# Seven blocks of a fused attention and two-MLP kernel: a table of start times becomes one written order, and the attention product of a head pair two matmuls

## The chip, the cores and the metric

The kernel runs on one core of one Trainium2 chip. The metric is the device time of one execution in microseconds (us). The profile was taken of one execution of the kernel before the change; its own time stands in the table below beside the median of three runs.

## What is computed

```python
def _attn_ref(q, k, v):                       # (8, 8, 576, 64) each
    q_s = q - np.max(q, axis=-1, keepdims=True)
    q_s = np.exp(q_s)
    q_s = q_s / (np.sum(q_s, axis=-1, keepdims=True) + 1e-09)
    k_s = k - np.max(k, axis=2, keepdims=True)
    k_s = np.exp(k_s)
    k_s = k_s / (np.sum(k_s, axis=2, keepdims=True) + 1e-09)
    kv = np.einsum('bhsd,bhse->bhde', k_s, v)
    return np.einsum('bhsd,bhde->bhse', q_s, kv)
...
    x = attn_out as 4608 rows of 512
    g = x @ w_gate;  val = x @ w_val           # 512 x 1536 each
    y = (g * sigmoid(g) * val) @ w_out         # 1536 x 512
    h = y @ w_in;  solu = h * softmax(h)       # 512 x 1024
    out = layernorm(solu) * g_ln @ w_out2      # 1024 x 512
```

All in float32. Each large product is made of three matmuls on float32r parts of its operands, high by high, high by low and low by high.

## The kernel before

The 4608 rows are nine **blocks** of 512. Block 0 runs in an opening that is written out by hand, and prepares block 1. Blocks 1 to 7 run in a steady loop. Block 8 and a tail (the second MLP, about 440 us) follow. The change touches blocks 1 to 7.

On TensorE a block is 36 **groups** of 12 matmuls of 512 columns: for each of the 12 slices i of the hidden width **g_i** (x times the gate weights, tile wg), **v_i** (x times the value weights, tile wv) and **o_i** (the product times the output weights, accumulated in the four banks y). g and v write in turn to four PSUM banks (the class Slots deals them out); so do the small tiles px and pk below. Before the change they run g_i, o_(i-2), v_i.

Between them stands the work for the block that follows, and other work that the block carries:
- **g and v**: ScalarE makes Silu of wg into a tile st (L891, three buffers). VectorE multiplies st by wv (L896), ScalarE rounds it to its high part a (L900, two buffers), VectorE subtracts for the low part (L902). Then o_i can run.
- **k and v of batch j+1**, four heads at a time: loads (kv_load, v_load), column maxima and subtraction on VectorE (kv_max_rows, kv_max_all), exp on ScalarE (kv_exp), 40 small matmuls into two pk tiles (kv_mm, L525), then scaling on VectorE and ScalarE into the 128x128 tiles kvh and kvl of each head pair, with the two heads' 64x64 blocks on the diagonal.
- **q of block j+1**: softmax over 64 (q_max, q_exp, q_norm), a transposing DMA (q_turn), then for each of four head pairs its parts qhl (q_split), and **x** of the pair (x_mm): three matmuls kvh by q high, kvh by q low, kvl by q high, for each batch that the 512 columns touch. A block that spans two batches has six matmuls a pair, a block in one batch three.
- **y of block j-1**: copied out of its banks (y_keep), seven forms made and stored (y_form).
- **w2**: one of eight pieces of the second MLP's weights is loaded raw (w2_raw), put together by two ScalarE instructions (L186, L187) and two on VectorE, and stored.
- **weights**: nine slices f of the gate and value weights are streamed from DRAM in each block, 1 MB each, through three buffers (stream_next), and the w2 piece takes a turn in them.

All DMAs are issued by SP, in program order; every engine runs its instructions in program order. Before the change the order comes from a table of start times: `at(t, n, ...)` puts a step behind the n-th of the 36 groups.

Of the kernel before, what the change touches and what calls it, by code (L numbers as in the profile page):

```python
# [18 lines left out]
P = 128  # L19
# [17 lines left out]
x2 g11 x3 x2 kvn v10 v11 s11 b8 x2 co5 o9 n2 g11 qnx co5 v10 v11 v11 v11 o10  # L37
""".split()


class Task:

# [1 line left out]
    current = None  # L44

    def __init__(self, f, a):
        self.f, self.a, self.g, self.done = f, a, None, False

    def step(self):
        before, Task.current = Task.current, self  # L50
# [13 lines left out]
    def next(self):  # L64
        self.step()
# [16 lines left out]
def attention_glu_solu_kernel(  # L82
# [46 lines left out]
    def f32(ap):  # L129
        return ap.bitcast(F32)  # L130
# [380 lines left out]
    def kv_mm(ps, pool, b, h0, u):  # L511
        pr = h0 // 2 + u
        need(pr in k_done if b == 0 else (b, h0) in kt_exp)
        pk = ps.tile([P, D + 1], F32, tag="gv", name="pk")
        heads = [2 * u + a for a in range(2)]
        if b:
            kt, vt = (t[b, h0][:, 0:NT_, :].rearrange("p (h c) d -> p h c d", c=LC) for t in (kt_t, vt_t))
            parts = [[(kt[:, h, c, :], vt[:, h, c, 0:D + 1]) for h in heads] for c in range(LC)]
            parts.append([(kt_t[b, h0][:, NT_ + u, :], vt_t[b, h0][:, NT_ + h, 0:D + 1]) for h in heads])
        else:  # L520
            kt, vt = kt_t[b, h0][1], vt_t[b, h0]
            parts = [[(kt[:, c, h, :], vt[:, h, c, 0:D + 1]) for h in heads] for c in range(KC)]
        for c, pair in enumerate(parts):
            for a, (kk, vv) in enumerate(pair):
                nc.tensor.matmul(  # L525
                    out=pk[a * D:(a + 1) * D, :], lhsT=kk, rhs=vv, start=c == 0, stop=c == len(parts) - 1
                )
        yield
        hi, lo = kv_parts[b % 2, pr]
        rs = stat.tile([P, 1], F32, tag="rs", bufs=4, name="rs")  # L530
        nc.vector.tensor_scalar_add(out=rs, in0=pk[:, D:D + 1], scalar1=1e-9)
        nc.vector.reciprocal(out=rs, in_=rs)
        yield
        diag = [slice(a * D, (a + 1) * D) for a in range(2)]
        for s in diag:
            nc.scalar.activation(out=hi[s, s], in_=pk[s, 0:D], func=AF.Copy, scale=rs[s])
        yield
        for s in diag:
            nc.vector.scalar_tensor_tensor(
                out=lo[s, s], in0=pk[s, 0:D], scalar=rs[s], in1=f32(hi[s, s]),  # L540
                op0=ALU.mult, op1=ALU.subtract,
            )
        kv_done.add((b, pr))

    kv_done = set()

    def segments(j):

# [107 lines left out]
    def q_turn(pool, j):  # L656

        n = BLOCKS[j][1] // 4
        w = tmp.tile([n, 2, 4 * H * D], U16, tag="yt", bufs=1, name="qw")
        parts = qt_t[j][1].bitcast(U16).rearrange("p c h (d w) -> p c h d w", w=2)  # L660
        wo = w.rearrange("p w (c h d) -> p w c h d", c=4, h=H)
        nc.vector.tensor_copy(out=wo[:, 0], in_=parts[:, :, :, :, 0])
        nc.scalar.copy(out=wo[:, 1], in_=parts[:, :, :, :, 1])
        qw_t[j] = wT = pool.tile([P, 2, 4, NPAIR, n], U16, tag="qt", bufs=1, name="qwT")
        nc.sync.dma_start_transpose(
            out=wT.rearrange("e w c r p -> e (w c r) p"), in_=w.rearrange("p w n -> p (w n)")
        )

    def q_split(pool, j, pr):

        wT, n = qw_t[j], BLOCKS[j][1]
        z = pool.tile([P, n], F32, tag="z", bufs=1, name="z")
        for half, copy in enumerate((nc.vector.tensor_copy, nc.scalar.copy)):
            copy(
                out=halves(z)[half].rearrange("e (c p) -> e c p", c=4), in_=wT[:, half, :, pr, :]
            )
        qh, ql = q_parts(pool, n)
        nc.scalar.copy(out=qh, in_=z)
        nc.vector.tensor_tensor(out=ql, in0=z, in1=f32(qh), op=ALU.subtract)
        qT_t[j, pr] = (qh, ql)  # L680

    xs = {}

    def x_tiles(xpool, j):
        xs[j] = [
            xpool.tile([P, KD, BLOCKS[j][1]], F32R, tag=f"{n}{j % 2}", name=n)
            for n in ("xh", "xl")
        ]

    def x_mm(ps, j, pr):  # L690
        qh, ql = qT_t.pop((j, pr))
# [36 lines left out]

    def tasks_of(j):

        t = {}
        b = j + 1
        if b < B:
            for n, (load, rows, sub, exp, mm) in enumerate(((0, 2, 5, 9, 11), (12, 17, 20, 24, 26))):
                h0 = n * HG  # L740
                if n:
                    at(t, load, kv_load, b, h0)
                    at(t, load, v_load, b, h0)
                at(t, rows, kv_max_rows, att, b, h0)
                a = Task(kv_max_all, (att, b, h0))
                at(t, sub, a.next)
                at(t, sub + 1, a.finish)
                at(t, exp, kv_exp, b, h0)
                for u in range(2):
                    at(t, mm, kv_mm, ps_at, att, b, h0, u)  # L750
        at(t, 15, lambda: w2_raw[j - 1].start())
        at(t, 23, join_w2, j - 1)
        at(t, 24, parts_of_w2, j - 1)
        if j + 1 < NB:
            m = Task(q_max, (att, j + 1, ALLH, nc.vector, 2))
            n = Task(q_norm, (att, j + 1, ALLH, nc.vector, 2))
            at(t, 8, m.next)
            at(t, 9, m.next)
            at(t, 10, m.finish)
            at(t, 12, q_exp, j + 1, ALLH)  # L760
            at(t, 13, n.next)
            at(t, 14, n.next)
            at(t, 15, n.finish)
            at(t, 18, q_turn, att, j + 1)
            at(t, 24, x_tiles, ph1x, j + 1)
            for p in range(NPAIR):
                at(t, 27 + p, q_split, att, j + 1, p)
                at(t, 29 + p, x_mm, ps_at, j + 1, p)
            at(t, 27, kv_next, j + 1)
            at(t, 33, q_next, j + 1)  # L770
        y_forms_at(t, j - 1)
        for e, f in enumerate(STREAM):
            if f is not None:
                at(t, 3 * f + 2, stream_next, j, e)
        at(t, 24, store_w2, j - 1)
        at(t, 25, stream_next, j, STREAM.index(None))
        return t
# [49 lines left out]
    def y_form(j, n):  # L827


        i, x, with_ = Y_FORMS[n]  # L830
        of = lambda n, r: y_quarter(j, n, r)
        if with_:
            if x and with_[0]:
                yz[j] = att.tile([P, 2, KH, P], F32, tag="z", bufs=1, name="yz")
            y_sum(yz[j], of, x, with_)
            s = yz[j]
        else:
            s = of(*x)
        f = att.tile([P, 2, 2, KH * P], F32R, tag="qhl", bufs=2, name="yf")
        h, l = (f[:, n].rearrange("p q (k t) -> p q k t", k=KH) for n in range(2))  # L840
        nc.scalar.copy(out=h, in_=s)
        yield
        nc.vector.tensor_tensor(out=l, in0=s, in1=f32(h), op=SUB)
        nc.sync.dma_start(out=yf_dram[j, i], in_=f32(f))

    def y_forms_at(t, j):


        tasks = [Task(y_form, (j, n)) for n in range(7)]
        for n, g in enumerate((4, 6, 8, 11, 12, 14, 16)):  # L850
            at(t, g, tasks[n].step)
            at(t, g + 1, tasks[n].finish)

    acts = {}
# [15 lines left out]

    ys = {}

    def emit_o(j, i, start, stop):
        if start:
            for t in ps0.held.values():
                t.finish()
            ys[j] = [y_bank(k)[:, :BLOCKS[j][1]] for k in range(KD)]
        ah, al = acts.pop((j, i))
        wh, wl = weight(("wo", i))
        for k in range(KD):  # L880
            s = slice(k * P, (k + 1) * P)
            mm3(ys[j][k], wh[:, s], wl[:, s], ah, al, start, stop)
        if stop and j < NB - 1:
            for k in range(KD):
                y_keep(j, k)

# [7 lines left out]
    def v_rest(j, i, pv):  # L894
        st = acts[j, i]
        nc.vector.tensor_tensor(out=st, in0=st, in1=pv, op=ALU.mult)  # L896
        yield
        a = apool.tile([P, 2, BLOCKS[j][1]], F32R, tag="a", bufs=2, name="a")
        ah, al = a[:, 0], a[:, 1]
        nc.scalar.copy(out=ah, in_=st)  # L900
        yield
        nc.vector.tensor_tensor(out=al, in0=st, in1=f32(ah), op=ALU.subtract)  # L902
        acts[j, i] = (ah, al)
# [38 lines left out]
    class Slots:  # L942
# [4 lines left out]

        def tile(self, shape, dtype, tag, name):
            k = self.at % self.n
            if k in self.held and not self.held[k].done:  # L950
                self.held[k].finish()
            self.at += 1
            self.held[k] = Task.current
# [23 lines left out]
    def opening():  # L977
# [102 lines left out]
        nc.sync.dma_start(out=g_sb, in_=g_ln.rearrange("(c p) -> p c", p=P))  # L1080
        pend.append((0, NF - 1, False, True))

    opening()
    for j in range(1, NB - 1):
        block(j, range(NF), tasks_of(j))
    man.close()


# [415 lines left out]
```

## Time and profile before

| | |
|---|---|
| median of 3 runs | 1350.85 us (1350.08 to 1351.71) |
| the profiled execution's own time | 1350.75 us |
| its span, first to last instruction | 1349.0 us |
| TensorE matmul busy | 1333.8 us, 99% |
| VectorE busy | 874.4 us, 65% |
| ScalarE busy | 688.0 us, 51% |
| mean granted TensorE clock | 0.997 |

A matmul's record lasts longer than the step from one matmul to the next, because they are pipelined. What a matmul costs in a stream is read from the starts: the distance from one start to the next. The profile's waits say which engine waited for which; TensorE's own waits all lie in the opening and the tail.

### The profile page before, as it was taken

How to read it: one execution, taken by the hardware profiler on the slowest of the kernel's cores; microseconds unless marked ns; L12 is line 12 of the kernel's file. 1: busy time of each engine (PE TensorE's matmuls, PEld its weight loads, DVE VectorE, ACT ScalarE, POOL GpSimd, SP SyncE). 2: the span in 40 equal slices, each digit the busy share in tenths (PEclk: the TensorE clock that was granted, in tenths of full speed). 3: DMA queues.
4: the chain of work that ended last, by engine and by line, in shares of the span. 5: the costliest groups of instructions: out<-in, count | busy, mean ns of one | idle time of the engine just before them, and what ended most of it. 6: DMA issues, size and time to landing. Idle time of an engine off the chain costs nothing.

```text
span 1349.0 us, 17478 instructions
## 1 busy us (share of the span) xinstructions
PE 1333.8 (99%) x6646; PEld 1102.4 (82%) x6646; DVE 874.4 (65%) x1513; ACT 688.0 (51%) x967; POOL 34.7 (3%) x134
## 2 busy tenths in 40 slices
PE   7999999999999999999999999999999999999998
PEld 5778888888888888888888888888887888888887
DVE  6999566376376466467367445464288778778774
ACT  5877255245345345344345424442166766766764
POOL 2000000000000000000000000000000000000000
PEclk9999999999999999999999999999999999999999
DMA  9977575476465556564664653564376676686651
GB/s 231 339 264 273 175 240 160 125 238 170 131 216 166 157 192 182 161 196 141 191 206 126 249 182 116 183 234 179 121 184 185 165 204 173 163 200 179 164 141 40
DMA packets 239700, 247.57 MB, mean 184 GB/s; under 512 B 147840, under 2 KB 213376, under 8 KB 228608
## 3 DMA queue, kind: packets, MB, share of 16 engines
q1 hardware_dynamic: 239616, 246.45, 61.0%
q8 instruction: 52, 0.85, 0.3%
q14 instruction: 32, 0.26, 0.1%
HBM read 162.01 MB, written 59.24 MB: 164 GB/s over the span
## 4 chain that ended last, share of the span: by engine, by line
PE 93%; DVE 4%; SPq 1%; issue 1%; DMA 1%; ACT 0%; DVEq 0%; ACTq 0%
PE wg L858 7%; PE y L860 7%; PE y L858 7%; PE y L859 7%; PE wv L858 7%; PE wv L860 7%; PE wv L859 7%; PE wg L860 7%; PE wg L859 7%; PE y L1335 5%; PE y L1334 5%; PE y L1333 5%; PE h L858 4%; PE h L860 4%; PE h L859 4%; PE pk L525 1%
## 5 line engine op out<-in xcount | busy, mean ns | idle before, releaser
L900 ACT CAST a<-st 128x512 fp32r<-128x512 f32 x108 | 66.9, 620 | 332.7 <-DVE st L896 328.1
L896 DVE TENSOR_TENSOR st<-st,wv 128x512 f32<-128x512 f32 x108 | 74.2, 687 | 185.2 <-PE wv L860 183.1
L858 PE MATMUL wg<-xh,wgv 128*128 128x512 f32 x432 | 170.5, 395 | 0.0
L860 PE MATMUL y<-a,wo 128*128 128x512 f32 x432 | 168.5, 390 | 0.7 <-DVE wo L221 0.7
L858 PE MATMUL y<-a,wo 128*128 128x512 f32 x432 | 168.6, 390 | 0.0
L859 PE MATMUL wg<-xl,wgv 128*128 128x512 f32 x432 | 168.5, 390 | 0.0
L858 PE MATMUL wv<-xh,wgv 128*128 128x512 f32 x432 | 168.4, 390 | 0.0
L859 PE MATMUL y<-a,wo 128*128 128x512 f32 x432 | 168.2, 389 | 0.2 <-DVE a L902 0.2
L860 PE MATMUL wg<-xh,wgv 128*128 128x512 f32 x432 | 168.3, 389 | 0.0
L860 PE MATMUL wv<-xh,wgv 128*128 128x512 f32 x432 | 168.1, 389 | 0.0
L859 PE MATMUL wv<-xl,wgv 128*128 128x512 f32 x432 | 168.1, 389 | 0.0
L902 DVE TENSOR_TENSOR a<-st,a 128x512 fp32r<-128x512 f32 x108 | 74.7, 692 | 76.9 <-ACT a L900 76.7
L1333 PE MATMUL y<-w,zhl 128*128 128x512 f32 (+1 forms) x296 | 113.6, 384 | 0.0
L1334 PE MATMUL y<-w,zhl 128*128 128x512 f32 (+1 forms) x296 | 113.5, 383 | 0.0
L1335 PE MATMUL y<-w,zhl 128*128 128x512 f32 (+1 forms) x296 | 113.5, 383 | 0.0
L891 ACT ACTIVATE st<-wg 128x512 f32<-128x512 f32 x108 | 64.4, 596 | 63.6 <-PE wg L860 63.2
L860 PEld LDWEIGHTS y<-a,wo 128*128 128x128 f32 x432 | 81.1, 188 | 18.8 <-DVE wo L221 1.9
L858 PEld LDWEIGHTS wg<-xh,wgv 128*128 128x128 f32 x432 | 81.4, 188 | 17.1 <-issue 0.2
L860 PEld LDWEIGHTS wg<-xh,wgv 128*128 128x128 f32 x432 | 81.2, 188 | 17.2
L859 PEld LDWEIGHTS y<-a,wo 128*128 128x128 f32 x432 | 81.1, 188 | 17.2 <-DVE a L902 0.6
L860 PEld LDWEIGHTS wv<-xh,wgv 128*128 128x128 f32 x432 | 81.1, 188 | 17.0
L859 PEld LDWEIGHTS wv<-xl,wgv 128*128 128x128 f32 x432 | 81.1, 188 | 16.7
(254 smaller groups left out, 2438.2 us busy)
## 6 DMA issues: line engine op xcount, KB each, us to landing
wgv<-w_dram SPq DMA_DIRECT2D x64, 1024.0 KB, 5.3
yf_dram<-yf SPq DMA_DIRECT2D x56, 512.0 KB, 3.0
yh<-yf_dram SPq DMA_DIRECT2D x18, 896.0 KB, 4.9
yl<-yf_dram SPq DMA_DIRECT2D x18, 896.0 KB, 7.2
w_dram<-wgv SPq DMA_DIRECT2D x10, 1024.0 KB, 8.5
out_dram<-ot SPq DMA_DIRECT2D x35, 256.0 KB, 2.8
kt<-in_k_dram SPq DMA_DIRECT2D x14, 512.0 KB, 6.5
vt<-in_v_dram SPq DMA_DIRECT2D x56, 128.0 KB, 5.1
```

Of the source, the lines that this page charges most:

```text
L525: nc.tensor.matmul(out=pk[a * D:(a + 1) * D, :], lhsT=kk, rhs=vv, start=c == 0, stop=c == len(parts) - 1)
L858: nc.tensor.matmul(out=po, lhsT=wh, rhs=rh, start=start, stop=False, **k)
L859: nc.tensor.matmul(out=po, lhsT=wh, rhs=rl, start=False, stop=False, **k)
L860: nc.tensor.matmul(out=po, lhsT=wl, rhs=rh, start=False, stop=stop, **k)
L891: nc.scalar.activation(out=st, in_=pg, func=AF.Silu)
L896: nc.vector.tensor_tensor(out=st, in0=st, in1=pv, op=ALU.mult)
L900: nc.scalar.copy(out=ah, in_=st)
L902: nc.vector.tensor_tensor(out=al, in0=st, in1=f32(ah), op=ALU.subtract)
L1333: nc.tensor.matmul(out=po[:, s], lhsT=zh[:, c, :], rhs=wh[:, s], start=first, stop=False)
L1334: nc.tensor.matmul(out=po[:, s], lhsT=zh[:, c, :], rhs=wl[:, s], start=False, stop=False)
L1335: nc.tensor.matmul(out=po[:, s], lhsT=zl[:, c, :], rhs=wh[:, s], start=False, stop=last)
```

## The change

Blocks 1 to 7 no longer use the table. A list of step names, BLOCK_ORDER, is walked once for each block by a new function, steady: g, v, o as above; o10p, v11p and o11p are the block before's last groups; yk copies y out; y0 to y6 are its forms; m, a, e and kv are the column maxima, their subtraction, exp and products of a half of the heads (0 or 1); qm, qe, qn, qt, q and x prepare x of the next block; w2 is the piece of weights; kvl1, kvn and qnx are loads. A name that stands several times runs one step of its task each time. TensorE's groups now run g0, o10p, v0, o11p, g1, v1, g2, v2, g3, v3, g4, o0, v4, o1, g5, kv0, v5, o2, g6, o3, v6, o4, g7, o5, v7, g8, x0, v8, o6, kv1, g9, o7, v9, x1, o8, g10, x2, v10, g11, x3, o9, v11.

x of a pair is made by x_mm2. The q tiles hold the two parts of one head stacked: in the first tile head A's high part in the upper 64 rows and its low part in the lower, in the second tile head B's, the other way round. The kv tiles hold each head's kv stacked to match, so that one matmul of 128 rows gives high by high and low by high in one half of its output and high by low in the other. There are then two matmuls a pair and batch, into two px tiles; ScalarE copies the one half of each and VectorE adds the other.

```diff
+BLOCK_ORDER = """
+m0 v11p g0 o10p v11p g0 v11p v0 o11p a0 yk v0 yk g1 a0 y0 y0 v1 g1 v0 g2 v2 y0 y1 v1 y1 v1 v0 g3 qm g2 qm v3 y2 qm
+y1 y2 y3 y2 g3 e0 g4 y3 v1 qe v2 o0 y3 y4 v4 qn o1 y3 g4 v3 qn w2 y4 v2 v2 v3 y4 y5 y5 g5 v4 qn y5 y4 kv0 kv0 y6 w2
+v5 qt o2 g5 kv0 v3 kvl1 w2 qt v4 y6 g6 kv0 g6 v4 qt o3 y5 v5 y6 v6 v5 o4 q0 v5 m1 v6 v6 g7 a1 o5 q0 y6 g7 w2 a1 q0
+q0 e1 v7 v7 v6 g8 x0 v8 w2 q1 w2 v7 x0 q1 g8 o6 x0 v8 kv1 kvn x0 kv1 v7 q1 kv1 q1 q2 v8 x0 g9 g9 o7 kv1 q2 v9 x1 q2
+v8 x1 v9 q2 v9 q3 x1 q3 v9 o8 q3 w2 q3 g10 g10 x2 v10 x2 x2 g11 x1 x1 v10 x3 o9 x3 x3 v10 v10 qnx x2 x3 x3 v11 g11
+x2
+""".split()
...
+        own = (hi, lo) if b > 1 else (hi, hi)
+        for w, s, o in zip(own, diag, reversed(diag)):
+            nc.scalar.activation(out=w[s, s], in_=pk[s, 0:D], func=AF.Copy, scale=rs[s])
+            if b > 1:
+                nc.scalar.activation(out=w[o, s], in_=pk[s, 0:D], func=AF.Copy, scale=rs[s])
+        yield
+        for w, s, o in zip(own, diag, reversed(diag)):
             nc.vector.scalar_tensor_tensor(
-                out=lo[s, s], in0=pk[s, 0:D], scalar=rs[s], in1=f32(hi[s, s]),
+                out=w[s, o] if b > 1 else lo[s, s], in0=pk[s, 0:D], scalar=rs[s], in1=f32(w[s, s]),
...
+    def kv_twice(b, pr):
+
+        hi, lo = kv_parts[b % 2, pr]
+        A, B_ = (slice(a * D, (a + 1) * D) for a in range(2))
+        for (to, i, k), (of, m, n) in (
+            ((lo, B_, A), (lo, B_, B_)), ((lo, B_, B_), (hi, B_, B_)), ((lo, A, B_), (hi, B_, B_)),
+            ((hi, A, B_), (lo, A, A)), ((hi, B_, A), (hi, A, A)),
+        ):
+            nc.gpsimd.tensor_copy(out=to[i, k], in_=f32(of[m, n]))
+        nc.gpsimd.memset(f32(hi[B_, B_]), 0.0)
+        nc.gpsimd.memset(f32(lo[A, A]), 0.0)
...
-        qh, ql = q_parts(pool, n)
-        nc.scalar.copy(out=qh, in_=z)
-        nc.vector.tensor_tensor(out=ql, in0=z, in1=f32(qh), op=ALU.subtract)
-        qT_t[j, pr] = (qh, ql)
+        qs = q_parts(pool, n)
+        own = [slice(a * D, (a + 1) * D) for a in range(2)]
+        for x, s in zip(qs, own):
+            nc.scalar.copy(out=x[s], in_=z[s])
+        yield
+        for x, s, o in zip(qs, own, reversed(own)):
+            nc.vector.tensor_tensor(out=x[o], in0=z[s], in1=f32(x[s]), op=ALU.subtract)
+        qT_t[j, pr] = qs
...
+    def x_mm2(ps, j, pr):
+
+        qs = qT_t.pop((j, pr))
+        n = BLOCKS[j][1]
+        px = [ps.tile([P, n], F32, tag="gv", name="px") for _ in qs]
+        for a, (x, po) in enumerate(zip(qs, px)):
+            x, po = (t.rearrange("e (c p) -> e c p", c=4) for t in (x, po))
+            for b, _, s in segments(j):
+                need((b, pr) in kv_two)
+                nc.tensor.matmul(
+                    out=po[:, :, s], lhsT=kv_parts[b % 2, pr][a], rhs=x[:, :, s], start=True, stop=True
+                )
+        yield
+        xh, xl = (x[:, pr, :] for x in xs[j])
+        own = [slice(a * D, (a + 1) * D) for a in range(2)]
+        z = tmp.tile([P, n], F32, tag="st", bufs=3, name="xs")
+        for po, s, o in zip(px, own, reversed(own)):
+            nc.scalar.copy(out=z[s], in_=po[o])
+        yield
+        for po, s in zip(px, own):
+            nc.vector.tensor_tensor(out=z[s], in0=po[s], in1=z[s], op=ALU.add)
+        Task.current.free = True
+        yield
+        nc.scalar.copy(out=xh, in_=z)
+        yield
+        nc.vector.tensor_tensor(out=xl, in0=z, in1=f32(xh), op=ALU.subtract)
...
+        def value(i):
+            pv = proj("wv", j, i)
+            if i in STREAM and i != 2:
+                stream_next(j, STREAM.index(i))
+            yield
+            yield from v_rest(j, i, pv)
...
+        def convert():
+            stream_next(j, 2)
+            yield
+            w2_raw[j - 1].start()
+            yield
+            join_w2(j - 1)
...
+            store_w2(j - 1)
+            yield
+            stream_next(j, STREAM.index(None))
...
+        for name in BLOCK_ORDER:
+            if name in tasks:
+                tasks[name].step()
...
     for j in range(1, NB - 1):
-        block(j, range(NF), tasks_of(j))
+        steady(j)
+    late.pop().finish()
```

**TensorE, x of head pair 1 for block 5, in block 4.** kvh_80, kvl_81 are the pair's kv of one batch, kvh_96, kvl_97 of the next; 4x80 and 4x48 are 320 and 192 columns. Before:

```order
L860 MATMUL wg<-xh,wgv_4319 128x512
L699 MATMUL px<-qhl,kvh_80 128x4x80
L700 MATMUL px<-qhl,kvh_80 128x4x80
L701 MATMUL px<-qhl,kvl_81 128x4x80
L699 MATMUL px<-qhl,kvh_96 128x4x48
L700 MATMUL px<-qhl,kvh_96 128x4x48
L701 MATMUL px<-qhl,kvl_97 128x4x48
```

Now:

```order
L894 MATMUL wv<-xh,wgv_4280 128x512
L738 MATMUL px<-qhl,kvh_80 128x4x80
L738 MATMUL px<-qhl,kvh_96 128x4x48
L738 MATMUL px<-qhl,kvl_81 128x4x80
L738 MATMUL px<-qhl,kvl_97 128x4x48
L892 MATMUL y_4311<-a,wo_1216 128x512
```

Six matmuls have become four, and batches now alternate.

**ScalarE, around the w2 piece of block 4.** w2r3r is the raw piece; st<-wg is a Silu, yf a form's high part, a the high part of a product. Before:

```order
L900 CAST a<-st 128x512
L841 CAST yf<-yz 128x512
L891 ACT_TABLE_LOAD
L891 ACTIVATE st<-wg 128x512
L186 ACTIVATE w2r3r<-w2r3r 128x1024
L187 ACTIVATE w2r3r<-w2r3r,floor_bias 128x1024
L841 CAST yf<-yz 128x512
L900 CAST a<-st 128x512
L891 ACTIVATE st<-wg 128x512
```

Now (the Silu behind w2r3r is that of g5):

```order
L634 ACTIVATE qt<-qt 128x4x8x64
L926 ACT_TABLE_LOAD
L926 ACTIVATE st<-wg 128x512
L873 CAST yf<-yz 128x512
L936 CAST a<-st 128x512 x2
L873 CAST yf<-yz 128x512
L195 ACTIVATE w2r3r<-w2r3r 128x1024
L196 ACTIVATE w2r3r<-w2r3r,floor_bias 128x1024
L926 ACTIVATE st<-wg 128x512
```

The two instructions on the raw piece now stand directly ahead of g5's Silu; the piece's load stands on SP behind the load that waits for v4.

**SP, the loads of the second half of block 4.** wgv_4529 and wgv_4842 are slice 11 before and now, wgv_4671 and wgv_4801 slice 0 of the next block; kt and vt are k and v of the next batch. Before:

```order
L240 DMA wgv_4529<-w_dram 128x2048
L362 DMA kt<-in_k_dram 128x4x256
L347 DMA kt<-in_k_dram 64x2x64 x2
L380 DMA vt<-in_v_dram 128x4x64 x4
L347 DMA vt<-in_v_dram 64x2x64 x2
L240 DMA wgv_4671<-w_dram 128x2048
```

Now:

```order
L371 DMA kt<-in_k_dram 128x4x256
L356 DMA kt<-in_k_dram 64x2x64 x2
L389 DMA vt<-in_v_dram 128x4x64 x4
L356 DMA vt<-in_v_dram 64x2x64 x2
L249 DMA wgv_4801<-w_dram 128x2048
L249 DMA wgv_4842<-w_dram 128x2048
```

Slice 11 has moved behind k and v and behind slice 0, which waits for v9.

## Rows read from the trace of the kernel before

**Rows 1.** The page's part 1: busy time, share of the span, instructions.

```profile
PE 1333.8 (99%) x6646; PEld 1102.4 (82%) x6646; DVE 874.4 (65%) x1513; ACT 688.0 (51%) x967; POOL 34.7 (3%) x134
```

**Rows 2.** One block's stretch: PE, PEld, DVE, ACT, POOL busy (instructions), clock, DMA share, GB/s.

```profile
282.98:387.12 104.14, 104.14 (x537) 86.52 (x537) 61.01 (x116) 44.70 (x66) 1.20 (x10) 1.00 0.58 175
```

**Rows 3.** Timeline of TensorE around px, blocks 1, 3, 6, 7: start us, us.

```profile
236.25 0.22 PE L699 MATMUL px<-qhl,kvh 128*128 128x128 f32 x1
...
239.83 0.22 PE L699 MATMUL px<-qhl,kvh 128*128 128x128 f32 x1
...
441.15 0.28 PE L699 MATMUL px<-qhl,kvh 128*128 128x256 f32 x1
...
444.61 0.28 PE L699 MATMUL px<-qhl,kvh 128*128 128x256 f32 x1
...
754.23 0.36 PE L699 MATMUL px<-qhl,kvh 128*128 128x448 f32 x1
...
754.84 0.19 PE L699 MATMUL px<-qhl,kvh 128*128 128x64 f32 x1
754.87 0.27 PE L700 MATMUL px<-qhl,kvh 128*128 128x64 f32 x1
754.98 0.28 PE L701 MATMUL px<-qhl,kvl 128*128 128x64 f32 x1
...
757.94 0.36 PE L699 MATMUL px<-qhl,kvh 128*128 128x448 f32 x1
...
859.19 0.39 PE L699 MATMUL px<-qhl,kvh 128*128 128x512 f32 x1
...
859.87 0.39 PE L858 MATMUL wv<-xh,wgv 128*128 128x512 f32 x1
...
862.59 0.39 PE L699 MATMUL px<-qhl,kvh 128*128 128x512 f32 x1
```

**Rows 4.** Groups by line and form: busy us, mean ns; idle before, releaser.

```profile
L902 DVE TENSOR_TENSOR a<-st,a 128x512 fp32r<-128x512 f32 x108 | 74.7, 692 | 76.9 <-ACT a L900 76.7
L805 ACT COPY yt<-y 128x512 f32<-128x512 f32 x18 | 10.6, 586 | 11.6 <-PE y L860 11.5
L536 ACT ACTIVATE kvh<-pk,rs 64x64 fp32r<-64x64 f32 x56 | 17.3, 309 | 28.1 <-DVE rs L532 16.6 <-PE wg L860 10.2 <-DVE rs L531 0.9
L891 ACT ACTIVATE st<-wg 128x512 f32<-128x512 f32 x108 | 64.4, 596 | 63.6 <-PE wg L860 63.2
L531 DVE TENSOR_SCALAR rs<-pk 128x1 f32<-128x1 f32 x28 | 4.3, 154 | 0.4
L532 DVE RECIPROCAL rs<-rs 128x1 f32<-128x1 f32 x32 | 5.3, 164 | 1.1
```

**Rows 5.** Timeline of SP, block 3: start us, us to issue.

```profile
375.29 0.32 SPq L844 DMA_DIRECT2D yf_dram<-yf  x1
375.71 0.37 SPq L240 DMA_DIRECT2D wgv<-w_dram  x1
377.67 0.32 SPq L844 DMA_DIRECT2D yf_dram<-yf  x1
378.08 0.39 SPq L175 DMA_DIRECT2D w2r2r<-in_moe_w_in_dram  x1
```

**Rows 6.** The tile w2r2r: its ScalarE instructions, and us from issue to landing.

```profile
L186 ACT ACTIVATE w2r2r<-w2r2r x1: 1132/1132/1132, 407.7 to 407.7; 128x1024 f32<-128x1024 f32 x1
L187 ACT ACTIVATE w2r2r<-w2r2r,floor_bias x1: 1204/1204/1204, 408.7 to 408.7; 128x1024 uint32<-128x1024 uint8 x1
...
DMA to landing us min/median/max: 7.8/7.8/7.8
```

**Rows 7.** Landing of Rows 5's load wgv, its second store, all wgv loads of 175:900.

```profile
DMA to landing us min/median/max: 6.4/6.4/6.4
...
DMA to landing us min/median/max: 5.7/5.7/5.7
...
DMA to landing us min/median/max: 4.7/5.2/7.6
```

## What I predict, and why

> **What bounds the kernel now.** I read the page's first part, then one block by itself, then TensorE's starts one by one, because the share of busy time does not tell whether there is anything to win. TensorE is busy 99% of the span, VectorE 65%, ScalarE 51% [rows 1]. In one block period of 104.14 us, TensorE is busy in all 104.14 us, at the full granted clock of 1.00, which is the 2.4 GHz level; VectorE works 61.01 us and ScalarE 44.70 us of it [rows 2]. So in blocks 1 to 7 nothing that TensorE waits for can be shortened. A reordering alone gains nothing there; it can only lose. What can gain is work taken off TensorE, and the change takes off some: matmuls of x. The rest of the argument is one saving and a list of the places where the new order could make TensorE wait.
>
> **TensorE's prices.** A group of 12 matmuls takes 862.59 - 859.87 = 2.72 us, or 0.227 us for 512 columns. From one px to the next lies one such group, so a pair's px costs the distance less 2.72: 0.68 us with all columns in one batch (859.19 to 862.59), 0.74 with 256 and 256 (441.15 to 444.61), 0.86 with 128 and 384 (236.25 to 239.83), 0.99 with 448 and 64 (754.23 to 757.94) [rows 3]. The pure columns, 3 x 0.227, are 0.68; the rest is a price of short matmuls: two with 64 columns start 0.11 us apart (754.87 to 754.98) where their columns are worth 0.03. The mean of the four is 0.82. With four pairs in each of seven blocks, x costs 28 x 0.82 = 22.9 us now.
>
> **What x costs after.** Two matmuls a pair carry 512 columns each: 2 x 0.227 = 0.45 us, and no less. The bound above gives each short piece the 0.11 us: with 448 and 64, 448 columns take 0.20 (754.23 to 754.43) and 2 x (0.20 + 0.11) = 0.62. A short piece now always stands behind a long one, and there the trace shows a 64-column matmul that took 0.03 us (754.84 to 754.87) [rows 3]. I am therefore nearer to the lower end and take 0.50: 28 x 0.50 = 14.0 us (12.7 at 0.45; 16.7 with 24 pairs at 0.62 and the four of one batch at 0.45). The saving is 22.9 - 14.0 = 8.9 us, bounds 6.2 and 10.2.
>
> The Trainium skill, page "TensorE: Matmul & The Clock Gate", section on LDWEIGHTS, prices a load of 128 weight columns at 128 / 1.2 = 107 ns; the 0.11 us just read agrees. By it four loads (0.43 us) hide under 0.45 us of columns, and the sum would end at 1350.75 - 10.2 = 1340.6 us. That a load does hide there no row here shows.
>
> **What is added, and what covers it.** VectorE gets three more instructions a pair (two additions into the half tiles, one more subtraction for q), each like the 0.692 of L902: 4 x 3 x 0.69 = 8.3 us a block, so 69 us. ScalarE gets two copies and one more cast a pair, like L805's 0.586, 4 x 3 x 0.586 = 7.0 us, and eight more writes of kv at 0.309, 2.5 us: 54 us [rows 4]. Both stay far below a block of some 103 us, and TensorE covers them; without that cover they would cost up to 18 us a block. GpSimd gets 28 small copies and fills once, in block 1; x0 comes 25 groups, 68 us, later, so even 1 us each would hide. Nothing of it is on the path unless a single step comes late. The extra steps sit where the order is densest, so I went through the new order place by place, adding prices ahead of each group of TensorE. Four places are tight; by the same sums the rest have over 2 us.
>
> 1. g6 and the w2 piece. The two ScalarE instructions on the raw piece stand ahead of g5's Silu, and g6 writes the PSUM bank that this Silu empties (four banks, taken in turn). The piece's load is the third DMA that SP issues behind v4's end, 0.8 us after it by the spacing of rows 5. There, a load, a store and the piece's load land 382.1, 383.4 and 385.9 (issue plus 6.4, 5.7 and 7.8 us) [rows 5 to 7]: in order, 0.5 MB 1.3 us and 1 MB 2.5 us behind the one ahead. So the slice's load lands 5.2 us after v4, the store 6.5, the piece 9.0. Then 1.13 + 1.20 us [rows 6] and the Silu's 0.60 [rows 4]: 11.9. TensorE gets to g6 after o1, g5, kv0, v5, o2: 4 x 2.72 + 1.5 = 12.4 (kv0 from rows 2: 104.14 less 36 x 2.72 and four px at 0.8 leaves 3.0 for two). Slack 0.5 us.
> 2. g11 and slice 11. Its 1 MB now goes behind slice 0's, both issued when v9 ends, behind k and v on SP. Slice 0 lands after 5.2 [rows 7]. Slice 11 follows at best 2.5 later, as the piece above did, and at worst 5.2, as if the two shared nothing: 7.7 to 10.4. I take the near end, since the piece is the same megabyte behind other traffic. TensorE needs it after x1, o8, g10, x2, v10: 3 x 2.72 + 2 x 0.50 = 9.2. Slack 1.5 us, at worst a wait of 1.2.
> 3. o7's low part stands on VectorE behind kv1's four small steps: 2 x (0.154 + 0.164) + 0.69 = 1.3 us after kv1 [rows 4], against g9's 2.72. Slack 1.4 us.
> 4. g0 of the next block needs x3: copies 1.2, addition 0.7, cast 0.6, subtraction 0.7, one more subtraction in the queue, about 4 us, against o9 and v11, 5.4. Slack 1.4 us.
>
> So the likeliest is that TensorE still never waits, and the time is 1350.75 - 8.9 = **1341.9 us** (the profiled execution's own time, 1350.75, is within 0.1 us of the median 1350.85). Block 8, the opening and the tail keep their order; I cost them at nothing.
>
> **The rivals.**
>
> *Slower: the w2 piece comes late.* If its load lands x us after v4's end, g6 waits x + 2.9 - 12.4 = x - 9.5 us in each of seven blocks. From x = 10.7 the waits eat the 8.9 us. With x = 11.5, 2.0 us a block, the result is 1341.9 + 14.0 = 1355.9 us. Behind the waiting ScalarE stand g5's Silu and all of kv0's writes. For it: three DMAs issued together rather than spread over 2.4 us as in rows 5, and the fourth form's store some 3 us behind. Against: they land in order, and 2.5 MB at the pace of rows 5 (3 MB from 375.29 to 385.9, 10.6 us) is 8.8 us. The Trainium skill, "DMA: Bandwidth & Descriptors", section on queues, rings and completion order, says that each DMA engine takes one queue's descriptors in order; by it the later store cannot delay the piece; without it, 1.3 us more and 0.8 us of wait a block, 1347.5 us.
>
> *Partly: small waits at g6 or g11.* 0.6 us a block, as slice 11 would cause if it landed at 9.8, is 4.2 us: 1346.1 us. For it: the worst end at g11, 1.2 us a block, would even cost 8.4 us, and the k and v loads ahead of it on SP may still be moving. Against: the longest of all such loads took 7.6 us [rows 7], which even issued 0.4 us after v9 is 8.0.
>
> *It does not do what it says.* The four matmuls cost what the six did, since x0 to x3 wait for q's or kv's stacked parts, made by more steps than before. All 28 px as long as now give 1350.75 us. Against: by the prices of rows 4, each pair's parts are ready over 3 us before its matmuls.
>
> **How the numbers follow.** No waits: 0.63, 1341.9 us, by the bounds of x's price 1340.6 to 1344.6. Small waits: 0.18, around 1346.1, 1343 to 1348.5. Late w2 piece, slower: 0.09, around 1355.9. As before: 0.05, 1350.75. Better than 1340.6, if the order also trims the few tenths that each px and pk cost at their edges: 0.05. For 8 in 10 the range takes the first case whole, and the second up to 1348.5, with a little room on both sides: 1340.0 to 1349.0. About 0.2% (2.7 us) is what a measurement of this kernel can tell from no change. Faster by more than that, below 1348.1: 0.63 + 0.05 + nearly all of 0.18 = 0.85. Within it: 0.06. Slower: 0.09.
>
> **What would show each step right or wrong.** TensorE in a block's stretch still fully busy, and the period shorter by 8.9 / 7 = 1.3 us, near 102.9. Four px matmuls a pair, the distance from px to px less the groups between near 0.50. The waits of TensorE in blocks 1 to 7 empty; a wait of wg for a Silu, with ScalarE idle before the w2 piece until its DMA, means the first rival, at g6; a wait of wg's weights for a DMA means g11. VectorE near 69 us and ScalarE near 54 us a block. I would be wrong if the period stayed near 104 with TensorE busy throughout: then matmuls themselves cost more in the new order, which nothing here lets me expect.

## The result: slower by 1.2%, and the profile after

| | before | changed |
|---|---|---|
| median | 1351.47 us (1350.08 to 1352.38) | 1369.97 us (1361.53 to 1371.76) |
| ratio | | 1.012 [1.009, 1.015] |
| the profiled execution, its span | 1350.75, 1349.0 us | 1361.53, 1359.8 us |

The forecast was 1341.9 us, with a range of 1340.0 to 1349.0. The six runs of the changed kernel lie in two groups, two near 1362 and four near 1370 us. The first trace is of the first group; the second group is explained in the fourth experiment. One execution of the first experiment's kernel took 1901.07 us at a mean granted clock of 0.653; its time below, 1342.87 us, is the median of the other three, and of all four it is the 1343.3 us that later expectations start from.

The page's first part, after, answers [rows 1]:

```profile
PE 1328.1 (98%) x6594; PEld 1095.3 (81%) x6594; DVE 923.6 (68%) x1585; ACT 738.4 (54%) x1087; POOL 46.0 (3%) x170
```

TensorE's work shrank, from 1333.8 to 1328.1 us, while the span grew by 10.8. So TensorE waits. A block's stretch in the changed kernel answers [rows 2] (us; PE, PEld, DVE, ACT, POOL busy with instructions; clock; DMA share; GB/s):

```profile
281.98:388.08 106.10, 103.55 (x530) 85.66 (x529) 67.93 (x126) 51.92 (x83) 1.20 (x10) 1.00 0.57 171
```

TensorE is idle for 106.10 - 103.55 = 2.55 us in a period that had no idle time before. The waits name the place: ScalarE's and TensorE's longest that concern the change (engine and line, released by; us in total, times, longest):

```profile
ACT yf L873 <- DMA yf_dram<-yf: 85.5, 15, 10.0
...
PE wv L892 <- DVE st L931: 15.8, 6, 2.8
```

Before, ScalarE's wait was 4.7 us, once, and TensorE had none of its kind. The second row is one wait in each of six blocks, always of the group v5, for VectorE's product of v4, which empties v5's PSUM bank. The first row is ScalarE held for a *store*. I followed one of these chains through block 3, engine by engine. SP first (start, us to issue), which answers [rows 5]:

```profile
384.26 0.32 SPq L249 DMA_DIRECT2D wgv<-w_dram  x1
384.63 0.90 SPq L877 DMA_DIRECT2D yf_dram<-yf  x2
```

A slice load that waits for v3's end (384.07) is issued, and only then the stores of the y forms 1 and 2. Form 1's parts had been ready since 374.7. Then ScalarE, VectorE and TensorE (in brackets the idle time ahead of an instruction and what ended it):

```profile
383.51 1.17 ACT L518 ACTIVATE kt<-kt 128x1152 f32<-128x1152 f32 x1
392.28 0.62 ACT L873 CAST yf<-yz 128x512 fp32r<-128x512 f32 x1 [7.61 <-DMA yf_dram<-yf]
392.81 1.91 ACT L634 ACTIVATE qt<-qt 128x2048 f32<-128x2048 f32 x1
394.74 1.28 ACT L926 ACT_TABLE_LOAD   x1
396.04 0.60 ACT L926 ACTIVATE st<-wg 128x512 f32<-128x512 f32 x1
...
394.75 2.29 DVE L640 TENSOR_REDUCE qs<-qt 128x32 f32<-128x2048 f32 x1 [0.40 <-ACT qt L634]
...
401.17 0.68 DVE L931 TENSOR_TENSOR st<-st,wv 128x512 f32<-128x512 f32 x1
...
401.90 0.50 PE L892 MATMUL wv<-xh,wgv 128*128 128x512 f32 x1 [2.76 <-DVE st L931]
```

The forms and q's parts share two buffers (the tag qhl). In the kernel before, a form's store was issued in the same step as the subtraction that completes it; in the changed kernel it is a step of its own. The fourth form's cast takes form 1's buffer, so it waits until form 1's store has landed. ScalarE takes its instructions in order: behind the cast stand q's exp and g4's Silu. VectorE needs that exp for q's sums, and the product of v4 stands behind them. It ends at 401.85, and v5 starts at 401.90, 2.76 us late.

### The profile page after: what moved, and what is told of

The parts are those of the page before. It is cut to its first block, busy times and chain, and to the rows that moved or that the text cites. A ratio compares the mean times of both kernels' runs of the same rounds, so it can differ in the third digit from the quotient of the medians.

```text
span 1359.8 us, 17609 instructions
## 1 busy us (share of the span) xinstructions
PE 1328.1 (98%) x6594; PEld 1095.3 (81%) x6594; DVE 923.6 (68%) x1585; ACT 738.4 (54%) x1087; POOL 46.0 (3%) x170
## 4 chain that ended last, share of the span: by engine, by line
PE 84%; DVE 7%; DMA 5%; ACT 1%; issue 1%; SPq 1%; ACTq 0%; DVEq 0%
PE wv L892 7%; PE wv L894 6%; PE wv L893 6%; PE y L893 6%; PE y L894 6%; PE y L892 6%; PE wg L892 6%; PE wg L893 6%; PE wg L894 6%; PE y L1474 5%; PE y L1476 5%; PE y L1475 5%; PE h L892 4%; PE h L894 4%; PE h L893 4%; DMA yf_dram<-yf 4%
## 5 line engine op out<-in xcount | busy, mean ns | idle before, releaser
L892 PE MATMUL wv<-xh,wgv 128*128 128x512 f32 x432 | 169.5, 392 | 15.9 <-DVE st L931 15.8
L892 PEld LDWEIGHTS wv<-xh,wgv 128*128 128x128 f32 x432 | 81.1, 188 | 33.6 <-DVE st L931 16.6
L894 PEld LDWEIGHTS y<-a,wo 128*128 128x128 f32 x432 | 81.1, 188 | 18.7 <-DVE wo L230 1.9
L893 PEld LDWEIGHTS y<-a,wo 128*128 128x128 f32 x432 | 81.1, 188 | 18.4 <-DVE a L938 2.0
L894 PEld LDWEIGHTS wv<-xh,wgv 128*128 128x128 f32 x432 | 81.1, 188 | 17.1
L892 PEld LDWEIGHTS y<-a,wo 128*128 128x128 f32 x432 | 81.1, 188 | 16.6 <-issue 0.2
```

The costliest lines, as they stand in the source:

```text
L892: nc.tensor.matmul(out=po, lhsT=wh, rhs=rh, start=start, stop=False, **k)
L893: nc.tensor.matmul(out=po, lhsT=wh, rhs=rl, start=False, stop=False, **k)
L894: nc.tensor.matmul(out=po, lhsT=wl, rhs=rh, start=False, stop=stop, **k)
```

## Experiments

**1. The stores ahead of the loads.** The edit moves names in BLOCK_ORDER; on every engine but SP the rows stay as they were.

```diff
-... a0 y0 y0 v1 g1 v0 g2 v2 y0 y1 v1 y1 v1 v0 g3 qm g2 qm v3 y2 qm
-y1 y2 y3 y2 g3 e0 g4 y3 v1 qe v2 o0 y3 y4 v4 qn o1 y3 g4 ...
+... a0 y0 y0 y0 v1 g1 v0 g2 v2 y1 v1 y1 y1 v1 v0 g3 qm g2 qm y2 qm
+y2 y3 y2 v3 g3 e0 g4 y3 v1 qe v2 o0 y3 y3 y4 v4 qn o1 g4 ...
```

> The changed kernel with one difference: on SP the stores of the y forms 0, 1, 2 and 3 stand ahead of the slice loads that wait for the ends of v1, v3 and v4, not behind them. All other engines keep their rows. Theory A (ScalarE is held for a y form's buffer until its store has landed; the store is late because it stands behind a slice load; the Silu and VectorE's product behind it come late, and v5 finds no free bank): ScalarE's 85.5 us of waiting for these stores falls under 15 us, TensorE's wait at v5 (6 times, 15.8 us in all) is gone, and the time is 1361.5 - 15.8 = 1345.7 us, between 1343 and 1349. Rival B (ScalarE and VectorE simply have too much in a row there: exp, two changes of ScalarE's table, 8.9 us of VectorE without a pause): ScalarE waits less for stores, but v5 still waits 2 us or more in each block, and the time stays at 1358 or above. Rival C (the stores take 7 us and more wherever they are issued, since the slice loads are moving): the wait shrinks to about half, some 1353 us.

Measured: 1342.87 us, ratio to before 0.9935 [0.9918, 0.9951]. TensorE has no wait left in blocks 1 to 7, and ScalarE waits for these stores once, 3.5 us. The chain of above, in this kernel's trace (its block 3 lies 6.32 us earlier, by the start of g5):

```profile
368.46 6.11 SPq L877 DMA_DIRECT2D yf_dram<-yf  x2
377.94 0.32 SPq L249 DMA_DIRECT2D wgv<-w_dram  x1
...
378.26 0.60 ACT L873 CAST yf<-yz 128x512 fp32r<-128x512 f32 x1
378.77 1.92 ACT L634 ACTIVATE qt<-qt 128x2048 f32<-128x2048 f32 x1
...
387.13 0.68 DVE L931 TENSOR_TENSOR st<-st,wv 128x512 f32<-128x512 f32 x1
...
392.76 0.50 PE L892 MATMUL wv<-xh,wgv 128*128 128x512 f32 x1
```

The cast stood at 392.28 - 6.32 = 385.96 by this clock and is now at 378.26, 7.70 us earlier; the product at 401.17 - 6.32 = 394.85 and now at 387.13, 7.72 earlier. It now ends at 387.81, 4.95 us before v5. So the delay of 7.72 us, less a slack of 4.95, is the wait of 2.76. Theory A holds. Rival B, that the two engines have too much to do there, falls: they do the same work in the same order. Rival C falls too: form 1's store lands 5.2 us after its issue here and form 2's 2.6, against 7.6 for form 1's behind the slice load.

**2 and 3. Each half of the change alone.** Run 2 puts the new kv parts, q_split and x_mm2 into the table of the kernel before; run 3 puts the old ones into the new order.

```diff
-                at(t, 29 + p, x_mm, ps_at, j + 1, p)
+                at(t, 29 + p, x_mm2, ps_at, j + 1, p)
```

```diff
-            add(f"x{p}", x_mm2, ps_at, b, p)
+            add(f"x{p}", x_mm, ps_at, b, p)
```

> The kernel before with its table of gaps, and of the change only the x of a head pair in two matmuls, with q's parts stacked and kv's parts written twice. In the changed kernel's trace a pair's x costs about 0.52 us against a mean of 0.78 to 0.82 before, so four pairs save about 1.0 us in each of seven blocks. Theory A (x is the saving, the order is the loss): 1351.0 - 7 = 1344 us, between 1342 and 1347, if the table's gaps have room for the added steps. Rival (the added steps of ScalarE and VectorE do not fit into the table, where a pair's parts are made in one go two groups ahead of its matmuls): TensorE waits for px or for a bank in the last third of each block, 0.5 to 2 us a block, and the time is 1347 to 1360 us. Rival B (the added work is what makes v5 wait) has nothing to wait for at v5 here and expects nothing else.

> The changed kernel's written order with the old x: three matmuls a batch, q's and kv's parts as before, one bank for px. Theory A: the stores stand where they stood in the changed kernel, so ScalarE's hold and TensorE's wait of about 2.6 us at v5 stay in six blocks; the x saving of some 7 us is lost: 1361.5 + 7 = 1368.5 us, between 1365 and 1372. Rival B (the work added by the stacked parts is too much for ScalarE and VectorE in this order): without it the wait at v5 is under 0.5 us a block, and the time is 1351 to 1355 us.

Measured: run 2, 1408.45 us, ratio 1.042 [1.041, 1.044], and run 3, 1380.05 us, ratio 1.021 [1.019, 1.023]. TensorE's longest waits that are not in the opening, of run 2 and then of run 3:

```profile
PE px L727 <- DVE qhl L707: 17.2, 23, 2.7
PE px L727 <- DVE xs L738: 11.7, 14, 1.4
...
PE wv L913 <- DVE xs L738: 3.3, 7, 0.6
```

```profile
PE wv L838 <- DVE st L877: 16.3, 6, 2.9
...
PE h L838 <- DVE hh L1302: 2.8, 1, 2.8
```

Run 2: my rival for it had the mechanism at a size far too small. In the table, q's parts and x are each written in one go, two groups apart, and x needs two banks: TensorE waits for q's parts and for VectorE's additions, 35.0 us with two smaller waits of these blocks (1.5 and 1.3 us); its busy time, 1358.1 us, is 30.9 above that of experiment 1, in part because the clock falls in every block. In block 2 it falls behind four short pauses in 7 us, the longest of 1.39 us (TensorE's px, then a stretch with columns as in [rows 2]):

```profile
343.09 0.50 PE L727 MATMUL px<-qhl,kvh 128*128 128x192 f32 x2 [0.78 <-DVE qhl L707]
343.81 0.49 PE L727 MATMUL px<-qhl,kvl 128*128 128x192 f32 x2 [0.22 <-DVE qhl L707]
...
347.43 0.50 PE L727 MATMUL px<-qhl,kvh 128*128 128x192 f32 x2 [0.38 <-DVE st L951]
349.31 0.53 PE L727 MATMUL px<-qhl,kvl 128*128 128x192 f32 x2 [1.39 <-DVE xs L738]
```

```profile
350.00:354.00 4.00, 4.00 (x12) 3.12 (x11) 2.43 (x4) 3.40 (x6) 0.00 (x0) 0.57 0.00 0
```

So the old table, as it stood, could not carry the two-matmul x. Run 3: the wait at v5 stays when the added work of x is gone (16.3 us in six waits), which refutes rival B a second time. The time came out 11.5 us above what I wrote, most of it from falls of the clock, at four of the six waits and once at a wait of 2.8 us at h, in the tail, and from that wait itself; I had counted neither.

**4. The changed kernel again,** unaltered.

> The changed kernel once more, unaltered. Its six runs fell into two groups, near 1362 us at a mean granted clock of 0.996 and 0.997, and near 1370 us at 0.989 to 0.991; the trace at hand is of the first group. If a trace of the second group comes, theory A' (TensorE's pause at v5 is long enough that the clock is sometimes lowered behind it) expects the granted clock below 1.00 in the few us behind the wait at v5, in several of the blocks, at the same waits of about 2.6 us. The rival (the waits themselves are longer, since the stores land later) expects a clock of 1.00 throughout blocks 1 to 7 and waits of about 4 us. If only the first group comes, the trace repeats the one at hand: 15 to 17 us of waits at v5.

Measured: 1367.98 us (1367.11 to 1370.5), ratio 1.012 [1.011, 1.014], and the trace is of the second group. Its waits at v5 are the same, 15.3 us in six. What differs is TensorE's busy time, 1334.8 against 1328.1 us for the same matmuls. Stretches around the wait of block 1, which ends at 189.59 (columns as above, the clock third from the end):

```profile
187.00:189.00 2.00, 0.04 (x2) 0.00 (x0) 1.97 (x5) 0.00 (x0) 0.60 (x5) 1.00 0.92 389
189.00:191.00 2.00, 1.41 (x3) 1.16 (x4) 2.00 (x3) 1.61 (x2) 0.00 (x0) 0.56 1.00 305
191.00:193.00 2.00, 2.00 (x7) 1.57 (x6) 1.90 (x7) 1.99 (x5) 0.00 (x0) 0.59 0.92 261
193.00:195.00 2.00, 2.00 (x11) 1.65 (x10) 2.00 (x3) 1.91 (x7) 0.00 (x0) 1.00 1.19 230
```

Around the end of a pause of 2.56 us the granted clock falls to its lower level, 1.2 GHz, and comes back a little over 3 us later; seven matmuls run in 2 us instead of eleven. In this trace that happens at four of the six waits, in the first one at none. Set beside the first trace, matmul by matmul, TensorE drops back by 1.2 to 1.6 us at each of the four, 5.5 us in all, of the 5.6 us by which the two executions differ. (The 1.7 us in the expectation of run 8 is the whole difference in busy time by four; the opening has a part in it.) Theory A' holds; the rival (longer waits) falls.

**5 and 6. Which store.** Run 5 only puts v3's load behind the stores of forms 1 and 2; run 6 only puts form 0's store ahead of v1's load.

```diff
-... g2 qm v3 y2 qm
-y1 y2 y3 y2 g3 ...
+... g2 qm y2 qm
+y1 y2 y3 y2 v3 g3 ...
```

```diff
-... a0 y0 y0 v1 g1 v0 g2 v2 y0 y1 v1 ...
+... a0 y0 y0 y0 v1 g1 v0 g2 v2 y1 v1 ...
```

> Of the four swaps on SP only one: v3's slice load goes behind the stores of the y forms 1 and 2; those of 0 and 3 stay behind the loads of v1 and v4. Theory A (the hold that decides is that of the fourth form's cast, 7.5 us, for the store of form 1): this hold goes and the one of 3.9 us for the store of form 0 stays; v5 does not wait, and the time is that of all four swaps, 1343.3 us, at most 1345. Rival (both holds push the same chain, so that each is worth a part): v5 still waits about 1 us a block, 1349 us or more.

> The other swap alone: the store of form 0 ahead of v1's slice load, those of forms 1, 2 and 3 behind theirs as in the changed kernel. Theory A: ScalarE's hold of 3.9 us goes, that of 7.5 us stays, v5 waits 2.6 us in six blocks as before, and the time is that of the changed kernel, 1361 to 1371 us according to how often the clock falls behind the wait. Rival (each hold is worth a part): the wait shrinks to about 1.5 us, 1355 us or less.

Measured: run 5, 1347.03 us, ratio 0.997 [0.996, 0.998], and run 6, 1367.52 us, ratio 1.012 [1.010, 1.014]. Run 6 is as expected: v5 waits 15.6 us in six, so the hold for form 0's store cost nothing. In run 5 the wait at v5 is gone, but the time is 4.2 us above experiment 1, more than I allowed. Form 3's store still stands behind v4's load, and so ahead of the w2 piece on SP. ScalarE waits for that store at a later cast and then 1.75 us more for the piece itself, and g5's Silu stands behind the piece. In block 3:

```profile
396.68 0.62 ACT L873 CAST yf<-yz 128x512 fp32r<-128x512 f32 x1 [5.48 <-DMA yf_dram<-yf]
399.05 1.16 ACT L195 ACTIVATE w2r2r<-w2r2r 128x1024 f32<-128x1024 f32 x1 [1.75 <-DMA w2r2r<-in_moe_w_in_dram]
...
401.20 0.60 ACT L926 ACTIVATE st<-wg 128x512 f32<-128x512 f32 x1
...
401.85 0.50 PE L892 MATMUL wg<-xh,wgv 128*128 128x512 f32 x1 [1.60 <-ACT st L926]
```

And in block 1:

```profile
192.16 0.60 ACT L926 ACTIVATE st<-wg 128x512 f32<-128x512 f32 x1
...
192.38 0.39 PE L894 MATMUL y<-a,wo 128*128 128x512 f32 x1
192.82 0.50 PE L892 MATMUL wg<-xh,wgv 128*128 128x512 f32 x1
```

That is the wait at g6 that my first rival described, with the sign that it named. The profile's waits list it in two blocks only (1.60 and 0.17 us), since a matmul's record outlasts the step to the next. By the starts g6 is late in each of blocks 1 to 6: in block 1 its first matmul comes 0.44 us behind the one ahead, not 0.23, and 0.06 us after g5's Silu has ended. Set beside experiment 1's trace, TensorE loses 0.3, 0.4, 1.7, 0.2, 0.3 and 0.4 us there, 3.3 of the 4.6 us by which the two traced executions differ; another 1.0 us lies in the opening.

**7 and 8. The same delay without a late store.** Nine and twelve needless VectorE instructions ahead of the product of v4, on top of experiment 1.

```diff
+            st = acts[j, i]
+            for _ in range(9 if i == 4 else 0):
+                nc.vector.tensor_tensor(out=st, in0=st, in1=st, op=ALU.max)
             yield from v_rest(j, i, pv)
```

> All four swaps, so no late store, and nine needless VectorE instructions on st (each the maximum of st with itself, which leaves it as it is) put ahead of VectorE's product of v4 in each of the seven blocks. In the trace with all swaps this product ends 4.95 us before v5 starts. Theory A (the changed kernel's wait is a delay of that product beyond this slack, whatever its cause): nine instructions of 0.60 to 0.69 us delay it by 5.4 to 6.2 us, v5 waits 0.5 to 1.3 us a block, and the time is 1347 to 1352 us with the clock at 1.00 behind these waits. Rival (the product has less slack than the trace shows, because other buffers hang on it): waits of 2 us and more, or waits at other groups too, over 1355 us.

> The same with twelve such instructions: a delay of 7.2 to 8.3 us, which is that of the late store in the changed kernel (7.7 us). Theory A: v5 waits 2.3 to 3.3 us a block, and, though no store is late, the time is that of the changed kernel: 1343.3 + 7 x 2.8 = 1363 us without falls of the clock, up to 12 us more if the clock falls behind each of the seven waits by what it cost in the trace of the changed kernel run again (1.7 us each). Rival (the falls of the clock belong to the transfers in flight, not to the pause): the same waits at a clock of 1.00 throughout, 1358 to 1366 us in every run.

Measured: nine, 1354.75 us, ratio 1.002 [1.001, 1.003], and twelve, 1378.09 us, ratio 1.020 [1.018, 1.021]. TensorE's waits at v5, of the first and of the second:

```profile
PE wv L892 <- DVE st L931: 9.9, 6, 1.7
```

```profile
PE wv L892 <- DVE st L931: 22.9, 6, 3.8
```

Three more instructions add 22.9 - 9.9 = 13.0 us in six waits, 0.72 us each; nine of them, 6.50 us, less a wait of 1.65 leaves a slack of 4.85, as read in experiment 1 (4.95). Both waits and both times came out above what I wrote, since I had sized the instruction at 0.60 to 0.69; and six blocks wait, not seven. The length of the pause parts the two kernels, not a late store and not the transfers, which are in flight at the pause in both: at six pauses of 1.65 us the clock never fell in the trace, at six of 3.82 us each time. Part of the first trace, where a pause ends at 294.99, then of the second, where one ends at 298.50 and the clock is down before it ends:

```profile
294.00:296.00 2.00, 1.01 (x4) 0.86 (x5) 1.90 (x4) 1.14 (x2) 0.15 (x1) 1.00 1.00 385
296.00:298.00 2.00, 2.00 (x10) 1.65 (x9) 1.90 (x8) 1.99 (x5) 0.00 (x0) 1.00 0.92 251
```

```profile
296.00:298.00 2.00, 0.00 (x0) 0.00 (x0) 1.83 (x4) 1.77 (x2) 0.00 (x0) 0.65 1.03 379
298.00:300.00 2.00, 1.50 (x4) 1.21 (x5) 2.00 (x3) 0.96 (x2) 0.00 (x0) 0.50 0.89 202
300.00:302.00 2.00, 2.00 (x6) 1.60 (x5) 1.90 (x7) 1.37 (x5) 0.00 (x0) 0.50 0.73 154
302.00:304.00 2.00, 2.00 (x7) 1.53 (x6) 2.00 (x3) 1.94 (x5) 0.00 (x0) 0.64 0.10 21
```

## Why the prediction was wrong

**What bounds the kernel: right.** A reordering could only lose, and TensorE's work was all there was to gain. With its waits gone (experiment 1) the kernel is 9.15 us faster than before, and 1.0 us from the 1341.9 forecast for "no waits". That it comes so near is in part luck: as the next paragraph shows, the seven blocks gave less than forecast, and the opening and the scatter of the runs made up for it.

**The saving: right in kind, a little too large.** Five periods, from one block's second kv product to the next block's, of before, of the changed kernel and of experiment 1, each in a fence of its own (sum of the stretches; busy sums; then means):

```profile
sum 521.44, PE 521.44 PEld 433.05 DVE 306.91 ACT 226.28 POOL 5.99; mean PE 104.29 PEld 86.61 DVE 61.38 ACT 45.26 POOL 1.20
```

```profile
sum 530.00, PE 516.88 PEld 427.87 DVE 342.20 ACT 262.08 POOL 6.60; mean PE 103.38 PEld 85.57 DVE 68.44 ACT 52.42 POOL 1.32
```

```profile
sum 516.67, PE 516.67 PEld 427.78 DVE 343.43 ACT 260.33 POOL 6.58; mean PE 103.33 PEld 85.56 DVE 68.69 ACT 52.07 POOL 1.32
```

TensorE's work falls by 0.91 and 0.96 us a block, so 6.4 to 6.7 us in seven, where I had 8.9 (bounds 6.2 and 10.2). From the first px of a pair to the matmul behind its last, the 28 pairs together take 21.9 us before (0.68 to 0.91 each) and 14.4 after (0.45 to 0.58); I had 22.9 and 14.0. The price after was nearly right. A pair in block 3, with two equal batches, takes 0.47 us:

```profile
429.24 0.40 PE L738 MATMUL px<-qhl,kvh 128*128 128x256 f32 x2
429.47 0.40 PE L738 MATMUL px<-qhl,kvl 128*128 128x256 f32 x2
429.71 0.40 PE L892 MATMUL wv<-xh,wgv 128*128 128x512 f32 x1
```

With 128 and 384 columns it is 0.58 (block 1), with 448 and 64 0.54 (block 6). The price before was too high, since it was the mean of four pairs that I had picked, read as a distance less one group: for 448 and 64 columns that made 0.99, where the six matmuls take 0.86 and the group around them the rest. Between 7.6 us of x and 6.7 us of period some 0.9 us stay unexplained. Of the 9.15 us of experiment 1, the two traced executions show 7.87: 0.63 in the opening and 7.24 behind it, which is nearer to the 7.6. The other 1.3 us are scatter: the execution traced before lay that much below the median of the runs beside experiment 1 (1352.02).

The Trainium skill ("TensorE: Matmul & The Clock Gate", section on LDWEIGHTS) gives a weight load as its columns divided by 1.2 in ns, so 107 ns for 128 columns; by an estimate from that, four loads (0.43 us) would hide under 0.45 us of columns. With 256 and 256 columns the trace nearly agrees (0.47), with 128 and 384 it does not (0.58): there the second load starts 0.11 us after the first (217.11 after 217.00), and the 128 columns ahead of it are worth 0.06.

**The added work: right.** VectorE at 68 and ScalarE at 52 us a block were forecast at 69 and 54, and neither is what TensorE waits for by its sum.

**The four tight places: no wait at three; at the first, the slack of 0.5 us was not there.** The 9.0 us for the w2 piece were too low. In run 5, whose SP order at this place is the one forecast (slice, store, piece), with no wait at v5 to cover it, the piece lands 9.7 to 9.9 us after v4's end, in block 3 11.4, and g6 waits, as above. Of the sum the first term was too small: the slice lands 5.9 to 6.2 us after v4's end, not 5.2; the store follows 1.2 to 1.3 us later (in block 3 2.7) and the piece 2.4 to 2.5, as forecast. The next store, issued 0.5 to 1.5 us behind the piece in run 5 and 6.6 to 8.0 in the changed kernel, makes no difference to those 2.4 to 2.5 us, so it does not delay the piece. In the changed kernel the late v5 gave g6 more time, and in experiment 1 the store no longer stands ahead of the piece, which then lands after 8.3 to 8.8 us; in block 3, its latest, ScalarE starts on it 395.66 - 385.91 = 9.75 us after v4's end, and g5's Silu ends 0.05 us before g6 starts:

```profile
395.66 1.11 ACT L195 ACTIVATE w2r2r<-w2r2r 128x1024 f32<-128x1024 f32 x1 [5.68 <-DMA w2r2r<-in_moe_w_in_dram]
396.67 1.19 ACT L196 ACTIVATE w2r2r<-w2r2r,floor_bias 128x1024 uint32<-128x1024 uint8 x1
397.77 0.58 ACT L926 ACTIVATE st<-wg 128x512 f32<-128x512 f32 x1
...
398.40 0.50 PE L892 MATMUL wg<-xh,wgv 128*128 128x512 f32 x1
```

**The step that failed: "by the same sums the rest have over 2 us".** Those sums went along the engines and took DMAs only as loads that somebody waits for. A store has a waiter too: whoever writes its source buffer next. The forms' stores had become a step of their own, behind the slice loads on SP, and I had even priced one there, the store that lands 6.5 us after v4's end, as something ahead of the piece. For form 1's store, behind the load at v3's end, the same price gives 384.07 + 6.5 = 390.6 us; it landed at 392.2. To have it I would have had to ask who takes that buffer next (the fourth form, one of two buffers), on which engine (ScalarE, in order), and what is queued there (exp, a Silu, and through VectorE's sums the product of v4). The slack at the end of that chain, 4.95 us, was indeed over 2; what I lacked was the delay that comes in at its beginning. And the cost of a wait was taken as its length, which leaves out the falls of the clock: with 15.8 us of waits the changed kernel's six runs lie 19 to 29 us above experiment 1.

**The rivals.** The slower case had the right form, a DMA late on SP that holds ScalarE. As the cause of the loss it was at the wrong place; at its own place it came true only once v5 no longer waited (run 5), at 0.2 to 0.4 us in five blocks and 1.7 in one, where I had priced 2.0 in each of seven. That its 1355.9 us lay near the changed kernel's 1361.5 to 1371.8 is luck.

## What to carry to other kernels

When steps are moved, list for each buffer who frees it; if a store frees it, the store's place in its DMA queue is part of that buffer's chain, and a store should not stand behind a load that waits for an engine's progress. Here four such swaps turned a loss of 1.2% into a gain of 0.65%, with every other engine's instructions in the same order; the one at v3's load alone gave 1347.03 us, the one at v1's nothing. And one part of such a change may have no value alone: the cheaper x lost in the old table, and the new order with the old x lost with its stores late. With the stores ahead, that order and the old x were not run.

## What the runs showed of the hardware

A pause of TensorE can cost more than its length, through the clock. Around pauses of 1.65 us the granted clock stayed at 1.00 (six in one trace, and the ten runs of that kernel lie within 1.9 us); around pauses of 2.5 to 2.9 us at v5 it fell in 13 of 24 (none, four, four and five of six in the traces of the changed kernel, of the changed kernel again, and of runs 3 and 6), so the same kernel has two times some 8 us apart; around 3.82 us it fell six times of six, in three of them for twice as long. A single fall set TensorE back by 1.2 to 1.6 us. The longest pause does not decide alone: in run 2's block 2 the clock fell behind four pauses that came close together, none above 1.39 us.

A store of 0.5 MB landed 2.6 us after its issue when nothing stood ahead of it in the queue (forms 0 and 2 in experiment 1's block 3), and 6.8 and 7.6 us after it right behind a 1 MB load just issued (forms 0 and 1 in the changed kernel's).
